# Halved row loads, split transposing loads and later activation loads in a kernel that sums a long convolution and a feed-forward

## The chip, the core and the metric

The kernel runs on one core of one Trainium2 chip. The core has a matrix engine (PE, with a queue of its own for weight loads), a vector engine (DVE), a scalar engine (ACT), GpSimd (POOL) and a sync engine (SP) that here only issues DMAs. Each engine works through its instructions in program order; DMAs that SP issues move data on the core's 16 DMA engines. The metric is the device time in microseconds, the median of several runs. Before the change it is 1239.23 us over three runs (1238.85 to 1240.17).

## The reference

```python
xn = layernorm(q)                                   # (2048, 1024), eps 1e-5
# A: short causal convolution on k, times v, long causal convolution, gate
k_shift = sum(k_pad[:, t:t + S] * shift_k[:, 3 - t] for t in range(4))
kv = k_shift * v
y = irfft(rfft(kv, 2 * S) * rfft(ssm_k, 2 * S))[:S] + kv * ssm_D
A = xn * y
# B: feed-forward, D = 1024, F = 3584
B = silu(xn @ w1) @ w2
out = q + A + B
```

All inputs and the output are float32; S is 2048 rows, D 1024 columns.

## The kernel before

**The feed-forward** is two large products, GEMM1 (`xn @ w1`) and GEMM2 (`h @ w2`). Every float32 operand is split into a high and a low float16 part, and each product runs as three matmuls, high by high, high by low and low by high (lines 985 to 987 in GEMM1, 1128 to 1130 in GEMM2). Most of GEMM1 and part of GEMM2 use a Strassen-like scheme: seven products of half blocks (P1 to P7) on sums of the quarters of x (A11, A12, A22, S1 to S4) and of w1 replace eight. The rows of x are worked through in two halves of eight tiles of 128 rows: `sp = 0` for the first, `sp = 1` for the second. GEMM1 begins with four plain units without the scheme; `units()` then runs 12 units for the first half of the rows and 14 for the second. A product there is four steps of three matmuls, so line 985 runs four times in each product and 80 times in the plain units.

**The convolution** is done by discrete Fourier transforms on PE (lines 1589, 1630 to 1632, 1818 to 1820) with the spectra multiplied on DVE, ACT and POOL. It runs beside GEMM1 and GEMM2, in eight groups of 128 channels.

**The order** of every engine's queue is made while the program is built. Each stage is a generator of operations with a guessed duration; the class `Order` holds all generators as streams, and at each step it issues the operation whose start time in its own clock, less the stream's bias, is the earliest (`run`). An operation is ready when what it reads and the place that it writes are free in that clock, plus a margin (`prepare`). For a load (`L`, line 336) the margin is 0.3 us by default, SP is taken to be busy for 0.4 us, and the bytes pass at 345 GB/s after 2.4 us. For a transposing load (`X`, line 340) SP is taken to be busy for 0.65 us plus the bytes at 240 GB/s. The chip then executes these queues in that order, each instruction waiting for semaphores.

**What the change touches:**

- `load_row` (line 522) loads one tile of 128 rows of x by 1024 columns in float32, 512 KB, into one of twelve buffers `xt`. `begin` issues rows 0 and 1, then the first pair of weight blocks in four pieces of 256 KB (`load_pair`), rows 2 and 3, the second pair, and rows 4 to 7; the other rows follow in `more_rows`. `ln_rows` takes the statistics of a row in two instructions of 512 columns each on DVE (line 546), combines them (line 548), takes a square root on ACT for rows 0 to 3, and normalises (line 585). `transposes` turns the normalised row on PE (line 604), and `split` makes the two float16 parts (ACT for the high part, line 362; DVE for the low one, line 354). `scales_w1` sums the squares of the weight pieces on ACT (tile `junk`), adds them over the partitions on PE (line 457) and derives a power of two; `factors_w1` splits the weights by it into tiles `wo`. Until the first rows have been turned, `keep_warm` fills PE with small matmuls of ones (line 1903), and `warm_up` before it (line 1896).
- `load_x` (line 1073) brings the second half of x to PE. `more_sums` has written the seven operands in row order to DRAM (`xsp`); `load_x` reads each back by one transposing DMA of 1 MB into one of the places `x0` to `x7`, in the order S3, A11, S2, A12, S1, S4, A22. A place becomes free when the last unit of the first half has used the operand in it (S3 goes to a place that is free earlier). The products of the last unit of the first half and the first unit of the second alternate, so PE keeps working while the operands are exchanged.
- `load_h` (line 1298) loads the activations h that GEMM1 left in DRAM, in tiles of 256 KB: 160 loads for the plain part of GEMM2 and 56 for its seven-product part. They go into twelve half slots `wo`, which GEMM1 uses for its weights, and all on SP's queue, where the convolution's loads, transposes and stores and the loads of w2 are too.

Of the kernel before, what the change touches and what calls it, by code (L numbers as in the profile page):

```python
# [21 lines left out]
S, D, F = 2048, 1024, 3584  # L22
HALF = S // 2
T2 = HALF // P
# [6 lines left out]
W = 512  # L31
# [18 lines left out]
PRODUCTS = {"P1": ("A11", "B11"), "P7": ("S3", "T3"), "P6": ("S2", "T2"), "P2": ("A12", "B21"),  # L50
            "P5": ("S1", "T1"), "P3": ("S4", "B22"), "P4": ("A22", "T4")}
# [5 lines left out]
PLAIN = [j for j in range(NF) if j // 2 not in PAIRS]  # L57
# [245 lines left out]
def h3_ffn_kernel(ctx, tc, x, kp, vs, fs, shift, dskip, w1, w2, cfwd, cinv, out):  # L303
# [6 lines left out]
    def rows(a):  # L310
        return a.rearrange("(b p t) d -> b t p d", b=2, t=T2)

    xr = rows(x)
# [7 lines left out]
    def size(a):  # L321
        n = 1
        for s in a.shape[1:]:
            n *= s
        return n
# [10 lines left out]
    def L(o, i, m=0.3):  # L336
        n = size(o) * o.shape[0] * mybir.dt.size(o.dtype)
        return Op("SP", 0.4, 0.1, lambda: nc.sync.dma_start(o, i), [i], [o], m, n)

    def X(o, i, m=0.3, k=None):  # L340

        n = size(o) * o.shape[0] * mybir.dt.size(o.dtype)
        k = k or (1.2 if i.space == bass.MemoryType.DRAM else 3.0)
        return Op("SP", 0.65 + n / 240e3, 0.1, lambda: nc.sync.dma_start(o, i, transpose=True), [i], [o], m, k * n)
# [36 lines left out]
    hsf = [{p[0]: dram.tile([4, P, NQ, 2, P], F16, name=f"hsf{p[0]}{b}") for p in PRODUCTS.values()} for b in range(2)]  # L381
    hs = [dram.tile([4, P, NF, 2, P], F16, name=f"hs{b}") for b in range(4)]
    ws = {i: {n: dram.tile([P, 2, KH, len(n) * P], F16, name=f"ws{i}_{n[0]}") for n in FACTORS} for i in range(2, NP - 1)}
    xsp = {p[0]: dram.tile([P, 4, KH, 2, P], F16, name=f"xsp{p[0]}") for p in PRODUCTS.values()}
# [134 lines left out]
    xts, xns, xo = {}, {}, [{}, {}]  # L519
    xtok = [{}, {}]  # L520

    def load_row(t):
        yield xts_r.ready
        xts[t] = xns[t] = xts_r.tile([P, D], uses=2)
        yield L(xts[t][0], xr[t // T2, t % T2])
        flag["xt", t].set()

    def ln_rows():
# [544 lines left out]
    def load_x():  # L1073
        yield flag["spilled"]
        for name in ("S3", "A11", "S2", "A12", "S1", "S4", "A22"):
            r = places[4 if name == "S3" else XPLACE[name]]
            yield r.ready
            xo[1][name], xtok[1][name] = r.tile([P, 4, KH, 2, P], F16)
            yield X(xo[1][name].rearrange("p i k h w -> p (i k h) w"), xsp[name].rearrange("p i k h w -> p (i k h w)"))
            flag["x", 1, name].set()  # L1080


# [52 lines left out]
    def uses2():  # L1135

        yield 0, "P1"
        for u in range(len(tiles2)):
            for n in ("P7", "P6", "P2", "P5") if u + 1 < len(tiles2) else ("P6", "P7", "P5", "P2"):
                yield u, n  # L1140
            if u + 1 < len(tiles2):
                yield u + 1, "P1"
            yield u, "P3"
            yield u, "P4"
# [153 lines left out]
    def load_h():  # L1298
        yield flag["factors"]
        for h in range(2):  # L1300
            for c, t in [(c, t) for ts in TOGETHER[h] for c in range(NC) for t in ts]:
                yield wo.ready
                flag["h", h, t, c].what = o, _ = wo.tile([P, 4, 2, P], F16)
                yield L(o, hs[t // 4][t % 4][:, PLAIN[4 * c]:PLAIN[4 * c] + 4])
                flag["h", h, t, c].set()
        for u, n in uses2():
            sp, q = tiles2[u]
            yield wo.ready
            flag["h2", u, n].what = o, _ = wo.tile([P, NQ, 2, P], F16)
            yield L(o, hsf[sp][PRODUCTS[n][0]][q])  # L1310
            flag["h2", u, n].set()

    def squares_w2():
# [551 lines left out]
    def begin():  # L1865
        for t in (0, 1):
            yield from load_row(t)
        yield from load_pair(0)
        for t in (2, 3):
            yield from load_row(t)  # L1870
        yield from load_pair(1)
        for t in range(4, 8):
            yield from load_row(t)
        add(more_rows(), 0.05)
        add(more_pairs(), 0.05)
# [44 lines left out]
    add(spill_w1(), 0.0)  # L1920
    add(feed_forward(), 0.0)
    add(load_x(), 0.06)
    add(load_h(), 0.05)
    add(room(), 0.05)
    add(change(), 0.1)
# [43 lines left out]
```

## Time and profile before

| | before |
|---|---|
| median of 3 runs | 1239.23 us (1238.85 to 1240.17) |
| profiled execution | 1239.78 us |
| its span on the core | 1237.8 us |
| granted clock of PE | 0.999 |
| HBM read and written | 171.46 MB, 88.34 MB |
| issue to landing of the 512 KB loads of x, median | 7.1 us |
| issue to landing of the h loads (`wo<-hs`), median | 3.6 us |

All durations come from one profiled execution, taken by the hardware profiler; its span counts from the first to the last instruction. In the timeline a row gives the start in us, the time in us (of several merged instructions from the first start to the last end), the engine, the line, the operation, the tile written and the tiles read with their shapes, and the count; in square brackets stands how long the engine was idle before it and what ended the wait. A list of waits gives the engine and line that waited, what it waited for, the total in us, the number of times and the longest. `SPq` is the queue of DMA issues on SP: the time of such a row is what the issue took on SP, not the transfer. A row of the windows view gives the window, its length, the busy time and count (x) of PE and of its weight loads, the granted clock, the DMA share and GB/s; restricted to one line it counts that line alone. Tile names leave buffer numbers out, so `x` stands for all eight places and `wo` for all slots.

### The profile page before, as it was taken

To read this page: it belongs to the slowest core of one execution; us is meant where nothing else is said; L and a number is where in the kernel's file an instruction comes from. 1 tells how busy PE (TensorE), PEld (TensorE's weight loads), DVE (VectorE), ACT (ScalarE), POOL (GpSimd) and SP (SyncE) were. 2 spreads that over 40 slices of the span, in tenths; PEclk is the share of its full clock that TensorE was granted. 3 is DMA by queue.
4 is the path that set the end of the run, shared out by engine and by line. 5 is a ranking of instruction groups with operands and counts; after the bars stand their busy time and mean duration, and the time that the engine had idled before them with its cause. 6 is when DMAs were issued, how large, how long until landed. Compare 5 with 4: busy or idle time off the path is not lost.

```text
span 1237.8 us, 16864 instructions
## 1 busy us (share of the span) xinstructions
PE 1227.2 (99%) x6044; PEld 597.6 (48%) x6044; DVE 1106.9 (89%) x1248; ACT 775.0 (63%) x1357; POOL 83.3 (7%) x93
## 2 busy tenths in 40 slices
PE   9999999999999999999999999999999999999998
PEld 8544444444444544445444544544454454444444
DVE  7999996996999779998999899799889979997992
ACT  7868897886687877659643832734363365536243
POOL 0000000000000000000000000001030130113114
PEclk9999999999999999999999999999999999999999
DMA  9598989899799889989876556489586775877767
GB/s 368 128 315 271 318 298 327 264 255 214 252 320 293 235 270 273 312 231 321 297 245 175 154 183 172 135 280 275 129 177 169 168 162 153 190 160 128 156 134 102
DMA packets 277700, 278.77 MB, mean 225 GB/s; under 512 B 85616, under 2 KB 204656, under 8 KB 276336
## 3 DMA queue, kind: packets, MB, share of 16 engines
q1 hardware_dynamic: 261888, 261.17, 70.0%
q0 software_dynamic: 15728, 16.52, 10.3%
q8 instruction: 47, 0.77, 0.3%
q14 instruction: 37, 0.30, 0.1%
HBM read 171.46 MB, written 88.34 MB: 210 GB/s over the span
## 4 chain that ended last, share of the span: by engine, by line
PE 79%; DVE 15%; issue 3%; ACT 1%; DMA 1%; SPq 0%; DVEq 0%; ACTq 0%
PE ff L1128 13%; PE ff L1129 13%; PE ff L1130 13%; PE ff L985 9%; PE ff L986 9%; PE ff L987 9%; DVE spec L351 3%; DVE ht L354 2%; DVE x L354 2%; PE ps L1630 2%; PE ps L1631 2%; PE ps L1632 2%; DVE tmp L351 1%; DVE hf L351 1%; DVE wo L354 1%
## 5 line engine op out<-in xcount | busy, mean ns | idle before, releaser
L1128 PE MATMUL ff<-x,wo 128*128 128x512 f16 x868 | 328.1, 378 | 1.8 <-ACT hf L362 1.2
L1130 PE MATMUL ff<-x,wo 128*128 128x512 f16 x868 | 328.1, 378 | 0.0
L1129 PE MATMUL ff<-x,wo 128*128 128x512 f16 x868 | 328.1, 378 | 0.0
L985 PE MATMUL ff<-x,wo 128*128 128x512 f16 (+1 forms) x808 | 302.7, 375 | 0.5 <-DVE hf L351 0.5
L987 PE MATMUL ff<-x,wo 128*128 128x512 f16 (+1 forms) x808 | 302.8, 375 | 0.0
L986 PE MATMUL ff<-x,wo 128*128 128x512 f16 (+1 forms) x808 | 302.8, 375 | 0.0
L351 DVE TENSOR_TENSOR spec<-spec 128x1024 f32<-128x1024 f32 (+2 forms) x232 | 260.0, 1147 | 2.3
L1130 PEld LDWEIGHTS <-wo 128*128 128x128 f16 x868 | 84.9, 98 | 101.6
L1129 PEld LDWEIGHTS <-wo 128*128 128x128 f16 x868 | 84.9, 98 | 101.1 <-issue 2.3
L1128 PEld LDWEIGHTS <-wo 128*128 128x128 f16 x868 | 85.8, 99 | 99.0
L987 PEld LDWEIGHTS <-wo 128*128 128x128 f16 x808 | 79.0, 98 | 92.4 <-DVE wo L354 0.5
L985 PEld LDWEIGHTS <-wo 128*128 128x128 f16 x808 | 80.5, 100 | 88.2
L986 PEld LDWEIGHTS <-wo 128*128 128x128 f16 x808 | 79.0, 98 | 89.2 <-issue 1.0
L351 DVE TENSOR_TENSOR tmp<-spec 128x2048 f32<-128x2048 f32 (+1 forms) x48 | 92.2, 1933 | 0.8
L354 DVE SCALAR_TENSOR_TENSOR ht<-hf,wsc,ht 128x1024 f16<-128x1024 f32 (+1 forms) x56 | 67.2, 1204 | 14.0 <-ACT ht L362 14.0
L362 ACT ACTIVATE spec<-spec 128x1024 bf16<-128x1024 f32 x32 | 33.7, 1053 | 65.9 <-DVE spec L351 65.9
L354 DVE SCALAR_TENSOR_TENSOR wo<-raw,wsc,wo 128x1024 f16<-128x1024 f32 (+1 forms) x56 | 63.9, 1146 | 3.5 <-ACT wo L362 3.4
L362 ACT ACTIVATE wo<-raw,wsc 128x1024 f16<-128x1024 f32 (+1 forms) x56 | 57.7, 1033 | 11.4 <-DVE raw L351 8.7
L354 DVE SCALAR_TENSOR_TENSOR sig<-kin,taps,sig 128x1024 f32<-128x1024 f32 x48 | 61.5, 1282 | 2.4 <-ACT sig L362 2.3
L362 ACT ACTIVATE ht<-hf,wsc 128x1024 f16<-128x1024 f32 (+1 forms) x56 | 60.7, 1085 | 4.1 <-DVE hf L351 2.6
L351 DVE TENSOR_TENSOR spec<-tmp 128x512 f32<-128x512 f32 (+1 forms) x80 | 61.0, 794 | 1.0
L348 POOL DMA_DIRECT2D out<-hf x44 | 38.5, 874 | 344.6 <-ACT hf L362 217.9
(191 smaller groups left out, 1697.1 us busy)
## 6 DMA issues: line engine op xcount, KB each, us to landing
wo<-hs SPq DMA_DIRECT2D x160, 256.0 KB, 3.6
hs<-ht SPq DMA_DIRECT2D x80, 256.0 KB, 4.8
raw<-in_w SPq DMA_DIRECT2D x28, 512.0 KB, 5.7
wraw<-in_w SPq DMA_DIRECT2D x24, 512.0 KB, 5.4
w2n<-in_w SPq DMA_DIRECT2D x24, 512.0 KB, 6.1
ws_T<-wo SPq DMA_DIRECT2D x22, 512.0 KB, 5.7
kin<-in_kp SPq DMA_DIRECT2D x16, 704.0 KB, 4.8
wo<-ws_T SPq DMA_DIRECT2D x22, 512.0 KB, 4.8
```

The costliest lines, as they stand in the source:

```text
L348: return Op("POOL", 1.1, 3.0, lambda: nc.gpsimd.dma_start(o, i, accum_op=ADD), [i], [o], m, 2.3 * n)
L351: return V(lambda: nc.vector.tensor_tensor(o, a, b, op=op), o, [a, b], **k)
L354: return V(lambda: nc.vector.scalar_tensor_tensor(o, a, s, b, op0=op0, op1=op1), o, [a, b] + ([] if isinstance(s, float) else [s]), **k)
L362: nc.scalar.activation(o, i, func, scale=scale, **kw)
L985: nc.tensor.matmul(o, w[:, 0, k], xf[:, :, k, 0], start=first and k == 0, stop=False, **kw)
L986: nc.tensor.matmul(o, w[:, 0, k], xf[:, :, k, 1], start=False, stop=False, **kw)
L987: nc.tensor.matmul(o, w[:, 1, k], xf[:, :, k, 0], start=False, stop=last and k == KH - 1, **kw)
L1128: nc.tensor.matmul(po, hx[:, n, 0, :], wc[:, n, 0, :], start=first and n == 0, stop=False, **kw)
L1129: nc.tensor.matmul(po, hx[:, n, 0, :], wc[:, n, 1, :], start=False, stop=False, **kw)
L1130: nc.tensor.matmul(po, hx[:, n, 1, :], wc[:, n, 0, :], start=False, stop=last and n == 3, **kw)
L1630: nc.tensor.matmul(o, cf[:, 0], h, start=i == 0, stop=False, **kw)
L1631: nc.tensor.matmul(o, cf[:, 0], l, start=False, stop=False, **kw)
```

## The change

Rows 0 to 3 of x are loaded by two DMAs of 512 columns each where there was one of 1024. Each operand of the second row half is loaded by two transposing DMAs of half the rows of its DRAM tile each, where there was one. The loads of h for GEMM2 get a margin of 3.0 us in the planner, where they had 0.3. No computation is added or removed; the planner makes the order of all queues anew from these operations.

```diff
@@ load_row
-        yield L(xts[t][0], xr[t // T2, t % T2])
+        for c in range(0, D, W if t < 4 else D):
+            cols = slice(c, c + (W if t < 4 else D))
+            yield L(xts[t][0][:, cols], xr[t // T2, t % T2, :, cols])
         flag["xt", t].set()
@@ load_x
-            yield X(xo[1][name].rearrange("p i k h w -> p (i k h) w"), xsp[name].rearrange("p i k h w -> p (i k h w)"))
+            for a in range(0, 4, 2):
+                yield X(xo[1][name][:, a:a + 2].rearrange("p i k h w -> p (i k h) w"),
+                        xsp[name][:, a:a + 2].rearrange("p i k h w -> p (i k h w)"))
             flag["x", 1, name].set()
@@ load_h
-                yield L(o, hs[t // 4][t % 4][:, PLAIN[4 * c]:PLAIN[4 * c] + 4])
+                yield L(o, hs[t // 4][t % 4][:, PLAIN[4 * c]:PLAIN[4 * c] + 4], 3.0)
                 flag["h", h, t, c].set()
...
-            yield L(o, hsf[sp][PRODUCTS[n][0]][q])
+            yield L(o, hsf[sp][PRODUCTS[n][0]][q], 3.0)
             flag["h2", u, n].set()
```

## The prediction

> **What bounds the kernel now.** I read the page's busy shares and the chain of waits first, then the view of who waited for whom on PE, then the timeline at both ends of the span.
>
> ```profile
> span 1237.8 us, 16864 instructions
> PE 1227.2 (99%) x6044; PEld 597.6 (48%) x6044; DVE 1106.9 (89%) x1248; ACT 775.0 (63%) x1357; POOL 83.3 (7%) x93
> ...
> PE 79%; DVE 15%; issue 3%; ACT 1%; DMA 1%; SPq 0%; DVEq 0%; ACTq 0%
> ```
>
> ```profile
> PE ft L604 <- DVE x L354: 1.5, 2, 1.2
> PE ff L1128 <- ACT hf L362: 1.2, 1, 1.2
> ...
> PE ff L1128 <- DVE hf L354: 0.6, 1, 0.6
> PE ff L985 <- DVE hf L351: 0.5, 1, 0.5
> PE py L1589 <- DVE sig L354: 0.4, 1, 0.4
> PE ps L1630 <- DVE spec L351: 0.3, 1, 0.3
> ```
>
> ```profile
> 15.56 0.27 PE L985 MATMUL ff<-x,wo 128*128 128x256 f16 x1
> ...
> 1232.58 0.27 PE L1130 MATMUL ff<-x,wo 128*128 128x256 f16 x1
> ```
>
> A busy PE alone proves little, since matmul ends are modelled. The waits prove it: between the first product of GEMM1 at 15.56 us and the last of GEMM2 at 1232.58, PE stood idle only 1.5 + 1.2 + 0.6 + 0.5 + 0.4 + 0.3 = 4.5 us. DMA and the SP queue release next to nothing on the chain that ended last (1% and 0%). What a change can gain is therefore the time before 15.56, those 4.5 us, and the tail of 1237.8 - 1232.85 = 4.95 us, which this diff does not edit. What it can lose has no such ceiling: the order of every queue comes from a planner, and the edits change what the planner sees.
>
> **The row loads.** Edit one replaces four DMAs of 512 KB by eight of 256 KB. Where it acts:
>
> ```profile
> 0.74 0.88 SPq L338 DMA_DIRECT2D xt<-in_x  x2
> 1.67 2.06 SPq L338 DMA_DIRECT2D x<-in_w  x4
> ```
>
> ```profile
> DMA to landing us min/median/max: 3.8/9.2/11.6
> ```
>
> ```profile
> GB/s 0 0 109 191 393 399 380 326 356 366 422 416 404 407 373 384 385 422 427 410 442 399 393 421 415 421 415 404 410 410 400 457 410 422 415 393 481 339 359 359
> ```
>
> ```profile
> 4.55 1.29 DVE L546 BATCH_NORM_STATS2 st<-xt 128x6 f32<-128x512 f32 x2 [3.45 <-DMA xt<-in_x]
> ...
> 6.00 1.23 DVE L546 BATCH_NORM_STATS2 st<-xt 128x6 f32<-128x512 f32 x2
> 7.26 0.21 DVE L548 BATCH_NORM_AGGREGATE ag<-st 128x2 f32<-128x12 f32 x1
> ...
> 8.50 0.81 DVE L585 TENSOR_SCALAR xt<-xt,ag,rstd 128x1024 f32<-128x1024 f32 x1
> ...
> 14.84 0.74 DVE L354 SCALAR_TENSOR_TENSOR wo<-x,wsc,wo 128x512 f16<-128x512 f32 x1
> ```
>
> ```profile
> 6.43 0.63 ACT L362 ACTIVATE junk<-x 128x512 bf16<-128x512 f32 x1 [4.20 <-DMA x<-in_w]
> 6.97 0.19 ACT L362 ACTIVATION_READ_ACCUMULATOR junk<-x 128x1 f32 x1
> 7.36 0.63 ACT L362 ACTIVATE junk<-x 128x512 bf16<-128x512 f32 x1 [0.20 <-DMA x<-in_w]
> ...
> 7.98 0.28 ACT L362 ACTIVATE nt<-ag,eps 128x2 f32<-128x2 f32 x1
> ```
>
> Row 0 is issued at 0.74 and lands 3.8 later, at 4.54, where DVE starts its statistics. The GB/s view cuts the first 30 us into 40 slices of 0.75 us; from the fifth on some 393 GB/s flow, so 256 KB take 262144 / 393e3 = 0.67 us. The first half can land at 4.54 - 0.67 = 3.87 and its statistics (0.65 us) fill the time until the second half. Row 1 is whole at 6.00 at the latest, since DVE starts it then without waiting; only its second half then remains: 6.00 + 0.65 + 0.21 = 6.86 for the end of the statistics, where it was 7.26 + 0.21 = 7.47. So 0.6 us come off there.
>
> The square root on ACT follows. It stood at 7.98, behind the second square sum of the weights (7.36), which waits for a DMA. I walked the planner's own arithmetic (a load's bytes at 345 GB/s, ready time minus bias) for these few operations: with halves the root is ready at 7.35 in its time and goes ahead of that second sum, by 0.01 of a microsecond. Then it can run when the first sum ends, 6.97 + 0.19 = 7.16, which is 0.82 earlier than 7.98; the normalisation at 8.50 moves to 7.7. If that near tie falls the other way, the root stays behind the same weight piece and nothing is gained.
>
> The first product at 15.56 needs the split weights too, which DVE wrote from 14.84. Their own chain is not touched by the edit:
>
> ```profile
> 9.11 0.83 PE L1903 MATMUL ff<-one 128*128 128x128 f32 x6
> 9.78 1.47 PE L604 MATMUL ft<-ident,xt 128*128 128x128 f32 x12
> 11.09 0.28 PE L457 MATMUL nm<-ss,one 128*128 128x4 f32 x2
> ```
>
> The weight norm on PE stands behind the first transposes in PE's order. These can move up only over the six fillers ahead of them, 9.78 - 9.11 = 0.67 us. DVE, whose queue holds both chains, is free 0.82 earlier. So PE's stream starts earlier by something between 0 (the weights decide) and 0.82; I take 0.6, near the 0.67 that the fillers allow. Four more issues at 0.88 / 2 = 0.44 us each on SP push the first weight pieces from 1.67 to 2.55, still ahead of the bytes queued before them (the stream is full until about 6). That cost is 0 under the cover of the transfers, and up to 0.88 without it. After 15.56 PE is fed without a gap but the listed ones, so 0.6 at the head is 0.6 at the end.
>
> **The transposing loads.** Seven loads of 1 MB become fourteen of half that size. Nothing shows a half-megabyte piece; the nearest rows are a quarter and a whole:
>
> ```profile
> 51.17 17.26 SPq L344 DMA_TRANSPOSE x<-s  x12
> ...
> 273.18 5.84 SPq L344 DMA_TRANSPOSE x<-xspA  x1
> ...
> 303.96 4.82 SPq L344 DMA_TRANSPOSE x<-xspA  x1
> ```
>
> ```profile
> x<-xspA SPq DMA_TRANSPOSE x1, 7.8
> ...
> x<-xspA SPq DMA_TRANSPOSE x1, 6.9
> ```
>
> ```profile
> 0.00:286.39 286.39, 151.17 (x408) 41.06 (x409) 1.00 0.88 281
> 0.00:317.47 317.47, 164.82 (x444) 44.58 (x445) 1.00 0.90 277
> ```
>
> A quarter holds SP 17.26 / 12 = 1.44 us; four make 5.75, against 4.82 to 5.84 for a whole. Splitting in two so costs between 0 and 1.44 us of SP per tile, some 0.2 by the mean of the two whole ones shown (5.75 - 5.33 = 0.42 for three further pieces, 0.14 each). Who waits: the first product that uses the second half's A11, and last A22. Line 985 runs 80 times in the four plain units and four times in each product; counted so, A11's first use is product 83 (408 runs before it) at 286.40, and A22's is product 92 (444) at 317.48. A11 was issued at 273.18 and landed 7.8 later, 280.98, so 5.4 us early; A22 at 303.96 + 6.9 = 310.86, 6.6 early. With 0.2 a piece both stay covered, and the gain is 0 as well, since PE waits for none of them. Stores of h that slip between the pieces (0.5 us of SP each) use up cover, not time. Value: 0; range 0 to the price in the last rival.
>
> **The later activation loads.** A margin of 3.0 for 0.3 lets the planner issue each of the 160 + 56 loads 2.7 us later in its time; other DMAs of the queue then go first.
>
> ```profile
> SPq L338 <- PE ff L1130: 274.0, 144, 7.4
> ```
>
> ```profile
> 1193.21 0.32 SPq L338 DMA_DIRECT2D wo<-hsfS  x1
> 1195.80 0.32 SPq L338 DMA_DIRECT2D wo<-hsfA  x1
> 1220.85 0.33 SPq L338 DMA_DIRECT2D ht<-out  x1
> ```
>
> ```profile
> wo<-hs SPq DMA_DIRECT2D x160, 256.0 KB, 3.6
> ```
>
> SP stood 274 us in front of these loads, 1.9 us each time, until PE freed a slot. A slot comes free every 1195.80 - 1193.21 = 2.59 us and there are twelve, so a load has 31 us until its tile is due and needs 2.7 + 3.6 of them. The longest stand of SP that could hold loads back, 25 us before 1220.85, has none behind it. So PE loses nothing by the margin; ACT and DVE get weights and signals earlier, which PE does not wait for. Value 0, and the range is that of a new order: any of the 4.5 us won, or new stalls of that size.
>
> Of rates: while whole rows arrive (slices five and six of the GB/s view, to 4.5 us) 393 and 399 GB/s flow; between 6.0 and 7.5 us, when only weights in pieces of 256 KB do (their first landings end ACT's waits at 6.43 and 7.36), 356 and 366. Should half rows run at the lower rate, 1 MB takes 1048576 / 361e3 = 2.90 us for 2.65, and row 1 is 0.25 later; that lies inside the 0 to 0.82. The Trainium skill (DMA: Bandwidth & Descriptors, section Bandwidth) has a rule that speaks against the halves: batch DMAs to 1 MiB or more for 75% of the peak. By that rule the lower rate holds and the sum would be some 0.25 higher, 1238.9; the trace agrees in direction, with 9% between the two rates, though the weights also come in shorter rows.
>
> **The sum.** Profiled span 1237.8 - 0.6 + 0 + 0 = 1237.2. The profiled execution took 1239.78, 1.98 outside its span, and the median is 1239.23, 0.55 below it. On the median: 1239.23 - 0.6 = 1238.6.
>
> **The rivals.**
>
> (a) No gain at the head. The weights' chain, not the rows, sets 15.56, or the near tie keeps the root where it was. For it: norm at 11.09 and split at 14.84 belong to the weights. Against: DVE does both chains in one queue and is freed earlier. Time 1239.2.
>
> (b) A luckier order. The new queues also remove about half of PE's idle 4.5 us: 1238.6 - 2.3 = 1236.3. For it: every stall is a wait for DVE or ACT, and 274 us of standing on SP are moved away from the loads that feed them. Against: none of these stalls waits for a DMA.
>
> (c) A worse order, slower. Where it happens:
>
> ```profile
> 1084.72 1.06 ACT L362 ACTIVATE spec<-spec 128x1024 bf16<-128x1024 f32 x1 [3.96 <-DVE spec L351]
> ```
>
> ACT's queue waited 3.96 us for a late spectrum of the convolution, the evacuation of a GEMM2 bank stood behind it, and PE lost its 1.2 us. With SP's other loads going first, the planner puts more such convolution work ahead of evacuations. It decides from the point where the spectrum is later than planned by more than the four banks cover; four more such places cost 4 x 1.2 = 4.8: 1238.6 + 4.8 = 1243.4. Against: it happened once in the whole span.
>
> (d) Pieces that pay a fixed price. If each further transposing piece costs a whole quarter's 1.44 us, A22 lands 7 x 1.44 = 10.1 later, 3.5 after 317.48: 1238.6 + 3.5 = 1242.1. It starts to decide at 6.6 / 7 = 0.94 us a piece. Against: four quarters cost no more than 0.9 above a whole.
>
> **How the numbers follow.** The forecast has 0.40, (a) 0.13, (b) 0.27, (c) 0.15, (d) 0.05. Predicted: 1238.6, its own range 1237.4 to 1239.2. The whole range reaches most of the way to (b) and (c): 1235.5 to 1242.6. A difference under 0.2% (2.5 us, so 1236.75 to 1241.7) can hardly be told from none here; faster than that is (b) with a little of the forecast, 0.28; slower (c) and (d), 0.20; between, 0.52.
>
> **What would show it.** Right: statistics on DVE from about 3.9, the root on ACT at about 7.2 ahead of the second square sum, the first L985 near 15.0, the last L1130 0.6 earlier, and PE's waits still 4 to 5 us in sum. Transposes on SP of about 2.7 us each, A22 landing before its first use. Wrong: the first L985 still at 15.5; or, the main danger, new PE waits for ACT hf or DVE of several microseconds between 330 and 1232.

## The result, and the profile after

| | before | after |
|---|---|---|
| median of 21 runs each | 1239.24 us (1238.31 to 1244.12) | 1241.45 us (1240.22 to 1247.01) |
| ratio after / before | | 1.0021, 95% interval 1.0014 to 1.0028 |
| profiled execution | 1239.78 us | 1240.22 us |
| its span | 1237.8 us | 1238.2 us |

The change made the kernel 2.2 us slower; the forecast was 0.6 us faster. The profiled execution of after is the shortest of its 21 runs and shows only 0.4 us of the loss, so a second profile was taken (E14 below). The ratios in the tables leave out two disturbed runs, of 1428 and 3368 us; the medians don't. The page of after, and its list of what PE waited for:

```profile
span 1238.2 us, 16874 instructions
PE 1227.2 (99%) x6040; PEld 597.1 (48%) x6040; DVE 1108.0 (89%) x1248; ACT 775.2 (63%) x1357; POOL 83.3 (7%) x93
```

```profile
PE ft L606 <- DVE x L354: 2.1, 3, 1.2
PE ff L987 <- ACT hf L362: 1.5, 2, 1.0
...
PE py L1823 <- DVE zl L354: 1.1, 2, 0.6
PE ft L606 <- issue: 0.7, 1, 0.7
PE ff L1132 <- DVE hf L354: 0.6, 1, 0.6
PE ps L1634 <- DVE tmp L351: 0.4, 1, 0.4
```

Busy time is that of before, as it must be; the line numbers are 2 or 4 higher. The three stalls of before at 535, 595 and 1086 us are gone, and others stand in their place: a new 1.5 us for ACT's evacuations (hf, the copies of finished sums out of the matrix engine's banks) in GEMM1, 1.1 for zl, an operand of the convolution.

**The head.** The timelines of DVE, ACT and PE after:

```profile
3.45 1.47 DVE L548 BATCH_NORM_STATS2 st<-xt 128x6 f32<-128x512 f32 x2 [2.35 <-DMA xt<-in_x]
...
6.27 1.33 DVE L548 BATCH_NORM_STATS2 st<-xt 128x6 f32<-128x512 f32 x2 [1.11 <-DMA xt<-in_x]
7.64 0.21 DVE L550 BATCH_NORM_AGGREGATE ag<-st 128x2 f32<-128x12 f32 x1
```

```profile
7.86 0.63 ACT L362 ACTIVATE junk<-x 128x512 bf16<-128x512 f32 x1 [5.62 <-DMA x<-in_w]
...
8.49 0.28 ACT L362 ACTIVATE nt<-ag,eps 128x2 f32<-128x2 f32 x1
```

```profile
16.89 0.27 PE L987 MATMUL ff<-x,wo 128*128 128x256 f16 x1
...
1234.59 0.27 PE L1134 MATMUL ff<-x,wo 128*128 128x256 f16 x1
```

The first half row is there at 3.45, 1.1 us earlier than a whole row was. The first half of row 1, however, is waited for until 6.27 (all of row 1 was there at 6.00 before, without a wait), and the first weight piece until 7.86 (6.43). The root stands right behind the first square sum, as forecast, but that sum is 1.43 late, so the root is at 8.49 for 7.98. The first product moves from 15.56 to 16.89. The windows view (its last three columns are the granted clock, the DMA share and GB/s) shows the bytes that did not come, first before, then after:

```profile
3.00:4.00 1.00, 1.00 (x7) 1.00 (x6) 0.00 (x0) 0.00 (x0) 0.00 (x0) 1.00 1.02 393
4.00:5.00 1.00, 1.00 (x7) 1.00 (x7) 0.45 (x1) 0.00 (x0) 0.00 (x0) 1.00 1.02 412
...
6.00:7.00 1.00, 1.00 (x7) 1.00 (x6) 1.00 (x3) 0.57 (x2) 0.00 (x0) 1.00 1.05 361
```

```profile
3.00:4.00 1.00, 1.00 (x7) 1.00 (x6) 0.55 (x1) 0.00 (x0) 0.00 (x0) 1.00 0.91 311
4.00:5.00 1.00, 1.00 (x7) 1.00 (x7) 0.88 (x3) 0.00 (x0) 0.00 (x0) 1.00 0.94 235
...
6.00:7.00 1.00, 1.00 (x7) 1.00 (x6) 0.73 (x2) 0.00 (x0) 0.00 (x0) 1.00 1.00 311
```

Between 4 and 5 us 235 GB/s flow where there were 412. PE's stream is here the sequence of its matmuls on one line, each compared with the same one before. From about 22 to 195 us it stands a constant 1.06 us behind.

**The exchange of operands.** Line 987's stream is 1.31 us late where the second half's first product begins, and 2.51 late at 335 us. The timelines of SP, ACT and PE after:

```profile
298.24 0.52 SPq L338 DMA_DIRECT2D hs<-ht  x1
298.86 5.79 SPq L344 DMA_TRANSPOSE x<-xspS  x2
304.74 5.52 SPq L344 DMA_TRANSPOSE x<-xspA  x2
310.31 1.74 SPq L338 DMA_DIRECT2D hs<-ht  x3
...
316.09 4.63 SPq L338 DMA_DIRECT2D hs<-ht  x4
```

```profile
313.16 1.15 ACT L362 ACTIVATE ht<-hf,wsc 128x1024 f16<-128x1024 f32 x1 [3.75 <-DMA hs<-ht]
...
326.00 1.15 ACT L362 ACTIVATE ht<-hf,wsc 128x1024 f16<-128x1024 f32 x1 [1.69 <-DMA hs<-ht]
```

```profile
316.70 0.38 PE L987 MATMUL ff<-x,wo 128*128 128x512 f16 x1 [0.98 <-ACT hf L362]
330.35 0.38 PE L987 MATMUL ff<-x,wo 128*128 128x512 f16 x1 [0.55 <-ACT hf L362]
```

Before, three stores of h went out ahead of S4 and A22:

```profile
295.14 2.52 SPq L338 DMA_DIRECT2D hs<-ht  x3
```

Now they stand behind both, at 310.31. ACT's split of h needs the buffer that the store empties and waits 3.75 us for it; the evacuation of a GEMM1 bank is queued behind that split, and PE waits 0.98 and 0.55 us for banks.

**The end.** The convolution's last matmul comes 8.35 us earlier (1205.33 for 1213.68), and the last two stores of the output land sooner (the DMA issues of before, then after; the last number is the us from issue to landing):

```profile
out<-hf SPq DMA_DIRECT2D x2, 128.0 KB, 3.9
```

```profile
out<-hf SPq DMA_DIRECT2D x2, 128.0 KB, 2.4
```

PE ends 2.01 us later, the tail behind it is 1.6 shorter (4.97 to 3.38), which leaves the profiled 0.4.

### The profile page after: what moved, and what is told of

Its sections match the earlier page's. It is cut to its first block, busy times and chain, and to the rows that moved or that the text cites. A ratio compares the mean times of both kernels' runs of the same rounds, so it can differ in the third digit from the quotient of the medians.

```text
span 1238.2 us, 16874 instructions
## 1 busy us (share of the span) xinstructions
PE 1227.2 (99%) x6040; PEld 597.1 (48%) x6040; DVE 1108.0 (89%) x1248; ACT 775.2 (63%) x1357; POOL 83.3 (7%) x93
## 3 DMA queue, kind: packets, MB, share of 16 engines
q0 software_dynamic: 15728, 16.52, 10.4%
## 4 chain that ended last, share of the span: by engine, by line
PE 33%; DVE 15%; issue 2%; DMA 1%; ACT 1%; SPq 0%; DVEq 0%; ACTq 0%
PE ff L1132 9%; PE ff L1134 9%; PE ff L1133 9%; DVE spec L351 6%; DVE tmp L351 3%; DVE x L354 2%; DVE sig L354 1%; PE ps L1636 1%; PE ps L1635 1%; PE ps L1634 1%; DVE spec L354 1%; PE py L1823 1%; PE py L1824 1%; PE py L1822 1%; DVE cm L354 1%
```

## The experiments

Medians stand with the count of runs, beside the kernel before on the same chip. Kernels with one run were profiled once and not timed further.

| | kernel | median (runs) | before (runs) | ratio, 95% interval |
|---|---|---|---|---|
| E1 | row halves alone | 1242.45 (11) | 1240.74 (33) | 1.0009, 0.9999 to 1.0019 |
| E2 | X pieces alone | 1243.23 (11) | same | 1.0021, 1.0013 to 1.0030 |
| E3 | margin alone | 1239.71 (11) | same | 0.9994, 0.9984 to 1.0003 |
| E4 | pieces and margin | 1244.21 (10) | same | 1.0031, 1.0015 to 1.0046 |
| E5 | pieces, cheaper for the planner | 1244.86 (5) | 1238.92 (9) | 1.0052, 1.0038 to 1.0066 |
| E6 | rows halved by partitions | 1251.86 (4) | same | 1.0097, 1.0082 to 1.0113 |
| E7 | halves of rows 0, 1 | 1243.29 (1) | same | |
| E8 | halves of rows 2, 3 | 1240.30 (1) | same | |
| E9 | row halves, order of before | 1242.30 (8) | 1238.59 (20) | 1.0029, 1.0019 to 1.0040 |
| E10 | X pieces, order of before | 1241.45 (7) | same | 1.0026, 1.0015 to 1.0038 |
| E11 | rows and margin | 1241.45 (10) | same | 1.0023, 1.0013 to 1.0033 |
| E12 | pieces, planned late | 1254.67 (4) | same | 1.0125, 1.0110 to 1.0140 |
| E13 | before again | 1238.98 (1) | 1238.69 (1) | |
| E14 | after again | 1244.19 (1) | same | |
| E15 | row 0 alone, order of before | 1242.32 (1) | same | |
| E16 | row 1 alone, order of before | 1241.23 (1) | same | |
| E17 | four X pieces, order of before | 1246.20 (4) | 1239.17 (17) | 1.0051, 1.0034 to 1.0069 |
| E18 | margin alone again | 1238.75 (12) | same | 0.9993, 0.9983 to 1.0003 |

### One part, or two parts, of the change

E1 has only the hunk of `load_row`, E2 only that of `load_x`, E3 only that of `load_h`, E4 the last two, E11 the first and the last.

> The row halves alone. Theory (the head loses): the half rows bring row 1 and the weights behind it about a microsecond later, every time; the first product starts near 16.9 us instead of 15.56, PE's stream stays about 1.1 us late to the end, the median is 1.0 to 1.3 us above the kernel before. Rival (one profile's luck): the late landing at the head was seen in one execution only; the first product starts near 15.0 and the time is 0.6 us below the kernel before.

> The transposing loads in two pieces alone. Theory (stores of h behind the pieces): first product at 15.56 as before; at the changeover between 295 and 335 us ACT waits for stores hs<-ht (some 7 us in sum), and PE waits for ACT hf once or twice, 1.5 us in sum; median 0.8 to 1.5 us above before. Rival (the changeover loses only together with the other edits, by a shifted plan): no PE wait for ACT hf there, median within 0.4 us of before.

> The later activation loads alone. Theory (a small gain in GEMM2): nothing changes before 540 us, PE's stream comes 0.3 to 0.6 us earlier at its end, the convolution's last matmul some 8 us earlier; median 0.2 to 0.7 us below before. Rival (a new order is as likely to lose): new PE waits in GEMM2 of 1 us or more in sum, median 0.5 to 2 us above before.

> The whole change without the row halves. Theory (the parts add up): the transposing pieces' 0.8 to 1.5 us less the margin's 0.2 to 0.7, so 0.3 to 1.0 us above before. Rival (the row halves cost nothing or the parts do not add): 2 us above before, as the whole change.

> The whole change without the transposing pieces. Theory (the pieces carry 1 us or more of the loss at the exchange of operands): no PE wait for ACT hf between 300 and 335 us, the time 0 to 1 us above before, so 1 us or more under the whole change's 2.2. Rival (the loss is only the new order of the second half of the kernel, whichever part makes it): 2 us or more above before, with waits of PE behind 500 us.

E1's first product is at 16.72, 1.16 late, and its stream 0.89 late until 195 us: the head's loss belongs to the row halves. Its ratio alone does not show a loss, since the interval reaches below 1. E2 leaves the first product at 15.55 and shows the exchange's loss without the other parts: the same late stores and a PE wait of 1.6 us for hf. Its median is 2.5 us above before, beyond the 0.8 to 1.5 expected; PE also loses 1.5 us near 199 us and waits 1.6 for zl at 683. E3 has no such wait at the exchange; in its profile the stall near 1086 is gone, a new one of 1.3 us for zl is there, and the convolution ends 4.3 us earlier. E4 waits 3.5 us for hf at the exchange and loses 4.6 there; the granted clock behind the wait is 0.50 over 3 us. E11's stream loses nothing there, yet its median is 2.9 us above before, against 0 to 1 expected: it misses. Its rival had 2 us or more with waits behind 500 us, and PE does wait 1.3 us for zl at 687; another 1.0 is lost near 199. The whole change without X pieces loses 0.23%, without row halves (E4) 0.31%, with both 0.21%. The parts don't add; the pieces, or the row halves with the margin, are enough for the whole loss.

### The head

```diff
@@ E6: load_row
+        for c in range(0, P, P // 2 if t < 4 else P):
+            part = slice(c, c + (P // 2 if t < 4 else P))
+            yield L(xts[t][0][part], xr[t // T2, t % T2, part])
@@ E7, E8: the change's loop, with
+        t < 2        # E7
+        2 <= t < 4   # E8
```

> Rows 0 to 3 in two DMAs each as in the change, but cut by partitions (64 rows of 4 KB) and not by columns (128 rows of 2 KB): as many DMAs and issues, packets of 4 KB. Theory (short packets): row 1 lands near 5.8 us and the first weight piece near 6.5, as before; first product 15.5 to 16.0. Rival (more DMAs and later issues): the first weight piece lands near 7.7 us as with the halves by columns, first product 16.7 to 16.9.

> Column halves for rows 0 and 1 alone. If the loss sits in the start of the stream: first weight piece near 7.7 us, first product 16.5 to 17. If it sits in rows 2 and 3: 15.6 or, with the earlier statistics of row 0, 15.0.

> Column halves for rows 2 and 3 alone. If the loss sits in the start of the stream: first product 15.5 to 16.0 as before. If it sits in rows 2 and 3: 16.5 to 17.

E6 tells nothing of row length, since its halves of 64 partitions are slow themselves: 245 GB/s from 2 to 8 us, the first product at 21.81. The Trainium skill (DMA: Bandwidth & Descriptors, Rules for kernel authors) advises against transfers to partition halves because they serialize. Here they also ran at well under the 393 GB/s of whole rows. E7 lands row 1 at 6.96 and has its first product at 17.63, E8 at 15.79. So the loss comes with rows 0 and 1; halves of rows 2 and 3, later in the stream, arrive 0.67 to 0.69 us apart, which is the full rate of 256 KB in 0.67.

The planner makes a new order in all of these. In E9, E15 and E16 it doesn't: one operation for the planner issues both halves, so the queues of PE, ACT, DVE and POOL are those of before, and SP's has only the further DMAs.

```diff
@@ L, E9, E15, E16
-        return Op("SP", 0.4, 0.1, lambda: nc.sync.dma_start(o, i), [i], [o], m, n)
+        def f():
+            c = o.shape[1] // parts
+            for p in range(parts):
+                cut = slice(p * c, (p + 1) * c)
+                nc.sync.dma_start(o[:, cut] if parts > 1 else o, i[:, cut] if parts > 1 else i)
+        return Op("SP", 0.4, 0.1, f, [i], [o], m, n)
@@ load_row
+        yield L(xts[t][0], xr[t // T2, t % T2], parts=2 if t < 4 else 1)
+        # E15: t == 0; E16: t == 1
```

> Rows 0 to 3 are loaded by halves, but both halves of a row are one operation for the planner, so every engine's queue is that of the kernel before, and SP's differs only by four further DMAs, each right behind its other half. Theory (the halves themselves arrive thinner on the chip): row 1 is whole about 1.0 us later than 5.8 us, the first weight piece about 1.2 later, the first product at 16.6 to 17.0, the time 0.9 to 1.4 us above the kernel before. Rival (the planner's other order of root, square sums and transposes costs the microsecond): first product within 15.5 to 16.0 and the time within 0.5 us of before.

> As e9, but row 0 alone in two halves (order of all queues as before). If the third DMA of the stream is late whatever it carries: row 1, now the third DMA and whole, lands at 6.5 to 7.0 instead of 5.8 and the first product is 0.7 to 1.1 later. If the loss belongs to the pieces of row 1: row 1 lands by 6.0 and the first product is at 15.5 to 16.0.

> As e9, but row 1 alone in two halves (order of all queues as before). If the third DMA of the stream is late whatever it carries: the second half of row 1, now the third DMA, lands at 6.5 to 7.0 and the first product is 0.7 to 1.1 later. If the loss needs halves of row 0 ahead: row 1 whole by 6.0 and the first product at 15.5 to 16.0.

E9: row 1 whole about 0.8 us late, the first weight piece at 7.50 (1.07 late), the first product at 16.47 (0.9 late). So the loss is made by the transfers; the planner's other order of root and square sums doesn't make it. Row 0 alone (E15) is worse than both: row 1, whole, is waited for until 8.03 (rows of DVE and PE, and the windows view):

```profile
8.03 1.29 DVE L552 BATCH_NORM_STATS2 st<-xt 128x6 f32<-128x512 f32 x2 [2.99 <-DMA xt<-in_x]
```

```profile
11.57 2.33 PE L610 MATMUL ft<-ident,xt 128*128 128x128 f32 x12 [2.63 <-issue]
```

```profile
11.50:14.00 2.50, 2.43 (x15) 2.46 (x15) 2.50 (x5) 1.54 (x5) 0.00 (x0) 0.61 1.09 389
```

The fillers that keep PE warm run out, PE stands 2.63 us, and the granted clock behind the pause is 0.61: twelve transposes take 2.33 us for 1.47. The first product is 3.45 late. E16, row 1 alone, loses less: first weight piece at 6.97, first product at 15.94 (0.38 late). Neither of the two sharp expectations was met: the DMA third in the stream is late in all three (E15 most, E16 least), but by different amounts, and in the kernel before it is not late.

E9 and E16 lose more behind the head. ACT and PE near 199 us, before and E9:

```profile
195.66 1.06 ACT L362 ACTIVATE junk<-raw 128x1024 bf16<-128x1024 f32 x1 [2.21 <-DMA raw<-in_w]
...
196.72 0.67 ACT L362 ACTIVATE x<-ff,wsc 128x512 f32<-128x512 f32 x1
```

```profile
198.80 1.06 ACT L368 ACTIVATE junk<-raw 128x1024 bf16<-128x1024 f32 x1 [4.45 <-DMA raw<-in_w]
...
199.86 0.67 ACT L368 ACTIVATE x<-ff,wsc 128x512 f32<-128x512 f32 x1
```

```profile
200.58 0.38 PE L991 MATMUL ff<-x,wo 128*128 128x512 f16 x1 [1.72 <-ACT x L368]
```

A square sum of weights waits for its load, an evacuation is queued behind it on ACT, and PE waits 1.72 us for the bank. Without the wait PE would have gone on at 198.86; shifted back by the 0.9 of the head that is 197.96 before, where the evacuation ended at 196.72 + 0.67 = 197.39. The cover, the time by which the evacuation was ahead of its use, was 0.57 us; the load came 3.14 us later (195.66 to 198.80), 2.24 without the head. The same stall, between 1.0 and 1.9 us of the stream, is in E1, E2, E7, E8, E9, E11 and E16, and a smaller one in E12 (0.4) and E17 (0.6); it is absent in both profiles of before and all but absent (0.2 us at most) in both of after. A late head is neither needed for it nor enough: E2's head is that of before, and E15, 3.45 us late, does not have it.

### The exchange of operands

```diff
@@ E5: X, and load_x with fixed=0.325 for each of two pieces
-        return Op("SP", 0.65 + n / 240e3, ...
+        return Op("SP", fixed + n / 240e3, ...
@@ E12: two pieces, and a later start for their stream
-    add(load_x(), 0.06)
+    add(load_x(), -2.0)
```

> The transposing loads in two pieces alone, but the planner charges each piece half of the fixed 0.65 us, so that two pieces cost SP in its clock what one load did; the planner then puts four stores hs<-ht between the pieces. Theory (order of the stores): the waits of ACT for hs<-ht and of PE for ACT hf between 295 and 335 us are gone; median 1.5 to 3 us below the pieces alone, within 1 us of before. Rival (the pieces' own price on SP): the same PE waits of 1.5 us or more remain there and the median stays 2 us or more above before.

> Transposing pieces alone, with the bias of their stream at -2.0 us for 0.06, so that the planner puts eight stores of h among them, ahead of A11, S1 and A22. Theory (ACT's split waits for a buffer whose store stands behind pieces on SP, and PE for that): the wait of ACT ht for stores stays under 1.5 us in all between 285 and 335 us and PE's wait for ACT hf there under 0.5 us; the price can move to late operands (PE waiting for the transposing loads), at most 2 us; without it the time is within 1 us of before. Rival (any order with pieces loses at that place for another reason): PE waits 1 us or more for ACT hf or ps there again, 2 us or more above before.

E5 does put stores among the pieces, and misses all the same; ACT and PE:

```profile
305.63 1.15 ACT L362 ACTIVATE ht<-hf,wsc 128x1024 f16<-128x1024 f32 x1 [3.95 <-DMA hs<-ht]
```

```profile
307.31 0.38 PE L1632 MATMUL ps<-sig,cfw 128*128 128x512 f16 x1 [2.57 <-ACT spec L362]
```

A store issued at 302.08, behind two pieces, is waited for until 305.6; now the convolution's evacuation stands behind that split. The clock over the next 3 us is 0.55, so PE's stream loses 4.4 us there for 2.57 of waiting. E12 removes ACT's wait for stores (none between 285 and 335 us) and PE's wait for hf there, as its theory says, but the operands come too late, which costs far more than the 2 us allowed for:

```profile
PE ff L985 <- DMA x<-xspA: 8.4, 2, 5.5
```

E10 and E17 leave every queue's order alone, as E9 did: one operation of the planner, at the price of the whole load, issues two or four transposing DMAs.

```diff
@@ X, E10 (E17: four)
+        def f():
+            for a, b in parts or [(o, i)]:
+                nc.sync.dma_start(a, b, transpose=True)
+        return Op("SP", 0.65 + n / 240e3, 0.1, f, [i], [o], m, k * n)
```

> The seven transposing loads in two pieces each, but both pieces are one operation for the planner at the price of the whole, so every engine's queue is that of the kernel before, and SP's differs only by seven further transposing DMAs, each right behind its other piece. Theory (the loss of the pieces comes from the planner, which charges each 0.65 us of SP more and lets the pieces pass the stores of h): no wait of ACT's ht for a store over 1 us around the exchange of operands, no PE wait for ACT hf over 0.5 us between 300 and 335 us, time within 0.6 us of before. Rival (pieces cost SP time or landing time on the chip): transposes of 2.9 us or more each on SP, stores of h late behind them, PE waiting 1 us or more there, the time 1 to 2 us above before.

> As e10, but each transposing load in four pieces, planned as one; the order of all queues as before. In e10 SP was 2.5 us late at the weight load raw behind A22 (312.54 for 310.01), ACT's split of it waited 5.0 us, and PE 1.9 for the evacuation behind. Theory (every further piece costs 0.3 to 0.4 us of SP, and raw passes it on to ACT and PE): raw issued 6 to 8 us later than before, PE waiting 4 to 7 us for ACT hf between 315 and 335 us or for the operands, the time 5 to 8 us above before. Rival (the 2.5 us came from that run, not from the pieces): raw within 3 us of before and the time within 3.5 us.

E10 refutes the planner as the only cause. SP, ACT and PE, before and E10:

```profile
310.01 0.58 SPq L338 DMA_DIRECT2D raw<-in_w  x1
```

```profile
314.86 0.72 ACT L362 ACTIVATE wo<-raw,wsc 128x512 f16<-128x512 f32 x1 [1.76 <-DMA raw<-in_w]
```

```profile
312.54 0.55 SPq L338 DMA_DIRECT2D raw<-in_w  x1
```

```profile
318.52 0.72 ACT L366 ACTIVATE wo<-raw,wsc 128x512 f16<-128x512 f32 x1 [5.03 <-DMA raw<-in_w]
```

```profile
330.26 0.38 PE L989 MATMUL ff<-x,wo 128*128 128x512 f16 x1 [1.87 <-ACT hf L366]
```

The load of the next weights, behind A22 on SP, is issued 2.53 us later; 0.40 of it was there before the first piece, from the later head of that run. ACT's split of it waits 5.03 for 1.76, and PE 1.87 for an evacuation behind. The profiled run is the longest of E10's seven (1243.31). Four pieces in place of two settle it (E17):

```profile
316.32 0.58 SPq L338 DMA_DIRECT2D raw<-in_w  x1
```

```profile
323.70 0.38 PE L989 MATMUL ff<-x,wo 128*128 128x512 f16 x1 [1.39 <-ACT hf L366]
334.15 0.38 PE L989 MATMUL ff<-x,wo 128*128 128x512 f16 x1 [2.52 <-ACT hf L366]
```

```profile
335.00:340.00 5.00, 5.00 (x18) 1.88 (x16) 5.00 (x6) 3.49 (x6) 0.00 (x0) 0.69 0.49 148
```

The load is 6.31 us later than before. Of this 0.87 was there before the first piece (0.27 from the head, 0.6 from the place near 199 us); the other 5.44 are 0.26 for each of 21 further pieces (E10: 2.13 over 7, 0.30 each). ACT waits 6.67 us, PE twice, 3.9 in sum where 4 to 7 were expected; behind the 2.52 the clock is 0.69. The time is 7.0 us above before, in the 5 to 8 expected.

### The same kernels again, and the margin

> The kernel before, profiled once more. Theory (its cover at two places is thin but holds: x of ACT at 199 us ends 0.6 us ahead of its use, the weight piece raw at 310 to 318 us in time for the evacuation): no PE wait for ACT x over 0.3 us near 199 us and none for ACT hf between 310 and 335 us; first product between 15.5 and 16.3. Rival (these waits come and go in every kernel): one of them of 1 us or more here too.

> The changed kernel, profiled once more; its first profile was the shortest of 21 runs. Theory: the first product again at 16.5 to 17.1 us, and now one of the two waits (ACT x near 199 us, ACT hf between 310 and 335 us) at 1 us or more, so that the last product ends 2.5 us or more behind the kernel before. Rival (the profile already showed the whole loss): again 2.0 behind, with no such wait over 1 us.

> The margin alone once more, over more rounds, as the one part that did not lose. Theory (its shorter end and its new waits cancel): within 0.1% of before on either side. Rival (it is a gain): 1 us or more under before with the interval clear of it.

E13's stream is within 0.15 us of the first profile of before at every place compared, with the same stalls. Before does not have the thin places by luck of one run. E14 is again 1.06 late at the first product, and 0.79 in the stream behind it; neither of the two waits named reaches 1 us (hf 0.8), so the expectation misses in the place. Nearly all of the further loss is in GEMM2, as the list of PE's waits and a window behind the longest one show:

```profile
PE py L1823 <- DVE zl L354: 4.1, 3, 2.0
```

```profile
892.60:895.60 3.00, 2.97 (x13) 1.83 (x13) 1.17 (x1) 0.45 (x2) 0.00 (x0) 0.53 0.06 22
```

PE waits for zl, the low part of the scaled inverse spectrum, at 679 (1.45), 892 (2.02) and 1107 us (0.62), and its last product ends 5.86 us later than before. The wait at 892 costs most: the clock behind it is 0.53, and PE's stream falls back 3.9 us there for 2.02 of waiting. The first profile of after waits for zl at two of these places only, 680 (0.43) and 1103 us (0.63), and loses 0.3 near 892. The two profiles, 1240.22 and 1244.19, stand on either side of the median.

E18 and E3 agree on the margin alone: 0.06 or 0.07% below before, each interval reaching 1.0003. Their profiles do not: PE's last product is 2.2 us later than before in E3, 0.45 earlier in E18. A gain isn't shown, and no kernel here clearly beats the one before.

## Why the prediction was wrong

**The view of the bound held.** Before was reproduced with its 4.5 us of stalls, and what could be won was small. "What it can lose has no such ceiling" was the right warning; the sum ignored it.

**The row loads: the failed step.** The term was -0.6 and measured +1.06 in the stream of the first profile and +0.79 in that of the second (0.9 with the order unchanged). Its first sub-step was right and more: the first half was there at 3.45, forecast 3.87. The sub-step that failed is "Row 1 is whole at 6.00 at the latest". It took the bytes to flow as before. They flowed at 235 to 311 GB/s for some microseconds, row 1 came whole at 6.9, its statistics ended at 7.85 instead of 6.86, and the first weight piece was 1.43 late, above the bound of 0.88 that the prediction had put on further issues. The rate question was asked: 361 for 393 GB/s, which the prediction made 0.25 us, a quarter to a third of the 0.8 to 1.1 by which row 1 and the head were late. The Trainium skill's rule there (DMA: Bandwidth & Descriptors, section Bandwidth) is to batch DMAs to 1 MiB or more. The runs agree with its sign at rows 0 and 1, but not at rows 2 and 3, whose halves came at full rate. The near tie of the root fell as worked out and was worth nothing: the square sum ahead of it waits for weights, and the weights were late. Rival (a) named that chain, but only as a missing gain.

**Head to end.** "0.6 at the head is 0.6 at the end" treats PE's stream as rigid. E16 and E9, 0.4 and 0.9 us late at the head, lost another 1.9 near 199 us, where a thin cover gave way (a late head alone doesn't do that, as E15 shows); and the end of after gave 1.6 back.

**The transposing loads: the second failed step.** The price on SP, 0.2 us a piece, was small but near (0.26 to 0.30), and both operands did stay covered: neither after, E10 nor E17 has a PE wait for them. What failed is "Who waits": it asked only for the readers of these loads. Everything that stands behind them on SP is late too. With the order of before it is the weights `raw` (2.1 us late, PE loses 1.87); in the planner's own order it is the stores of h, of which the prediction said that they "use up cover, not time". They used up 7.7 us of ACT's, in four waits, and 1.5 of PE's:

```profile
ACT ht L362 <- DMA hs<-ht: 7.7, 4, 3.8
```

**The margin.** Value 0, measured -0.4 and -1.0 us on the medians, with ratio intervals that hold 1: right alone. The stall at 1086 went, as rival (b) had it, and waits for zl came, as in (c).

**The rivals.** (c) described the mechanism that won, an evacuation behind a late operation on ACT's queue that costs PE a bank, but put it in GEMM2 with late spectra, where it was near 199 and 317 us with late DMAs. Its chance, 0.15, was too low: two of the three edits found such a place. In the second profile of after, though, most of the loss is in GEMM2 behind late spectra (zl, 4.1 us of waits), where (c) and the prediction's main danger had it; there PE waits for DVE itself, with no evacuation between them. In (d) the fixed price was wrong (0.3, not 1.44), and its point of decision, 0.94 us a piece, was that of the operands; for the weights behind them it lay below 0.30.

**What stays open.** Why the stream of row 0's halves runs thin from about 3.5 us, and more so when a whole row follows than when halves do, isn't explained; descriptor handling, the size of packets and the number of issues were not separated. Nor is it explained why the load at 188 us is later by more than the head in some kernels and not in others (in E9 an issue ahead of it on SP takes 1.97 us for 0.50 before, and the load lands 10.4 us after its own issue for 9.3), nor what makes the zl waits of after differ from run to run. How the 2.2 us of the median divide among the three places is known only for the two profiled runs.

## What to carry to other kernels

When a step on a queue gets longer, count what that costs everything behind it, loads and stores alike, and not only the readers of what it brings: for each, find the reader and its cover. Where PE is busy 99%, list the places where the other engines finish less than a microsecond ahead of it before moving anything; here there were at least three. Count a pause of PE at more than its length: in E14 a wait of 2.02 us cost 3.9 through the lower clock behind it. To tell a planner's reordering from the cost on the chip, issue the new pieces from one planned operation, so that every other queue keeps its order.

## What the runs showed of the hardware

- Two half rows at the start of the stream brought fewer bytes than whole rows: 235 GB/s between 4 and 5 us after the change, 412 before (in the second profile of after 249 between 5 and 6 us, 319 before), while halves two rows later came at full rate, 0.67 to 0.69 us apart (E8).
- With halves of 64 partitions 245 GB/s flowed between 2 and 8 us (E6), where whole rows brought 393 from 3 us on.
- Pauses of PE of 2.0 to 2.6 us were followed by a mean granted clock of 0.50 to 0.69 over windows of 2.5 to 5 us (E5, E7, E14, E15, E17). One of 1.87 us (E10) was followed by 1.00, and so was one of 2.39 us (E7, at 578 us), so the length alone does not decide. The Trainium skill (TensorE: Matmul & The Clock Gate, Part 1) puts the return to half clock behind an idle window of about 3.4 us. Here shorter pauses were enough.
- A transposing DMA of half a megabyte held SP 2.2 to 3.3 us after the change (median 2.9), a whole one 4.7 to 5.8 before. Summed over the seven operands, a further piece cost SP 0.25 to 0.4 us (E17, E10, after). Each piece landed 5.7 us after its issue (median) where a whole took 7.1 or 8.2 (medians of its two groups).
